# Attention and feed-forward on one core: scales from sums over partitions, and the last key tile's sigmoids as float16 parts lying over each other on partitions

## The chip, the cores and the metric

The kernel runs on one core of a Trainium2 chip. The metric is the device time of one execution, in microseconds, and lower is better. TensorE (PE in the profile) does the matmuls, VectorE (DVE) and ScalarE (ACT) the element-wise work, GpSimd (POOL) small scalings, and SyncE (SP) issues the DMAs.

## The reference, cut to what matters

```python
scores = (1 / sqrt(64)) * q @ k.transpose(0, 1, 3, 2) - log(448)      # q, k, v: (8, 12, 448, 64)
attn   = 1 / (1 + exp(-scores))                                       # a sigmoid, no softmax
x      = (attn @ v).transpose(0, 2, 1, 3).reshape(3584, 768)
h      = x @ w_in                                                     # 768 x 2048
g      = where(h > 0, h, exp(min(h, 0)) - 1)
out    = g @ w_out                                                    # 2048 x 768
```

All inputs and the output are float32.

## The kernel before, in words

A float32 matmul is replaced nearly everywhere by three float16 matmuls: each operand is scaled by a power of two and split into a high part (ScalarE, `nc.scalar.mul`) and a low part, the residual (VectorE, `scalar_tensor_tensor`), and high x high, low x high and high x low are accumulated. The helper `split` (L120) does both halves, so the profile shows them as L121 and L122 whatever the tile.

The work goes by batches (8) and within a batch by pairs of heads (6, `hp`). A pair's 448 keys are three tiles of 128 (`g` = 0 to 2) and a rest of 64 (`g` = NC = 3). For each tile there are `scores` (L384, into the PSUM tile `psc`), `soften` (the sigmoid L395 into `sg`, and for tiles 0 to 2 the split into `at`, L413 on ScalarE and L414 on VectorE) and `values` (L433: six float16 matmuls for a tile, each with 64 of the array's columns for one head, into `pav`). The rest tile has the 64 keys of both heads on one tile's 128 partitions: head 0 on 0 to 63, head 1 on 64 to 127. Its sigmoids stay float32, and one float32 matmul (L425) of 128x128 by 448 columns multiplies them with `vr`, in which the two heads' rest values stand as diagonal blocks, with zeros beside them; POOL makes `vr` (L360). The profile counts this matmul as two instructions. `finish` (L440, L441) splits `pav` into `xh` and takes its maximum.

`prepare` finds the powers of two for a later pair: absolute maxima along the rows of `rv`, the raw v, and of `raw`, which holds q and k (L300, L303; both show as L125), then the maximum over partitions in `magnitude`. That builds a diagonal matrix `dg` of the maxima, one for each of the three numbers (L105, VectorE), multiplies it with ones on TensorE (L110, 384 columns) so that each partition has all the maxima in a row, and reduces along the row (L112); L113 and L114 make a power of two of it. It returns in two further steps, `second` (the matmul and what follows) and `third` (the splits of q, k and v, and the DMA transpose).

Batch 0 (`EXACT` = 1) is done with float32 matmuls, while w_in is loaded and split beside it; w_out is loaded and split in batch 0's feed-forward and in the first pairs of batch 1. From batch 1 on the order on PE, ACT, DVE and SP is the order written (`manual_schedule`); before that a scheduler that simulates times orders the instructions. In the written order the pairs of batch b are mixed with the second feed-forward product of batch b - 1 (`moe2`, L529): `fill(n)` puts n steps of three matmuls between the parts of a pair. A batch has 96 such steps where b - 1 is even and 128 where it is odd, 16 or 21 for each pair. After the pairs comes the first product of batch b (`moe1`, L499), whose own scale goes through `magnitude` too (L457). One pair runs so:

```python
                for t in range(2):
                    p.scores(t)
                    p.soften(t)
                third()
...
                fill(gap)
                second = prepare_pair(n + 2)
                for t in range(2, NC + 1):
                    p.scores(t)
                    p.soften(t)
...
                fill(share - gap - tail)
                third = second()
                for t in range(NC + 1):
                    p.values(t)
                p.finish()
                fill(tail)
```

`gap` is 8 in a batch's first pair and 5 in the others, `tail` is 4 in its last pair and 0 in the others. In batch 1 the splitting of w_out (`step`) stands between the last `soften` and the second `fill` of the first three pairs. The output of a finished `moe2` tile leaves PSUM by L537.

Of the kernel before, what the change touches and what calls it, by code (L numbers as in the profile page):

```python
# [9 lines left out]
F16 = mybir.dt.float16  # L10
BF16 = mybir.dt.bfloat16
# [21 lines left out]
def attention_ffn(  # L33
# [64 lines left out]
    def magnitude(dst, mx, n):  # L98

        dg = sb.tile([P, n, P], BF16, tag="dg", name="dg", bufs=2)
        for i in range(n):
            nc.vector.tensor_scalar(dg[:, i], eye, mx[:, i : i + 1], None, op0=ALU.mult)  # L105

        def rest():
            pb = ps.tile([P, 512], F32, tag="pm", name="pb", bufs=3)
            row = pb[:, : n * P].rearrange("p (n x) -> p n x", x=P)
            nc.tensor.matmul(row, ones, dg, start=True, stop=True)  # L110
            al = sb.tile([P, n], F32, tag="al", name="al", bufs=2)
            nc.vector.tensor_reduce(al, row, axis=AX.X, op=ALU.max)  # L112
            nc.vector.tensor_scalar(al, al, TINY, None, op0=ALU.max)  # L113
            nc.vector.tensor_scalar(  # L114
                dst.bitcast(U32), al.bitcast(U32), 0x7F800000, None, op0=ALU.bitwise_and
            )
# [128 lines left out]
    def load_keys(dst, rest, src, b, h0):

        nc.sync.dma_start(
            dst.rearrange("p (h x) -> p h x", h=2),
            src[b, h0 : h0 + 2, :SM].rearrange("h (p c) d -> p h (c d)", c=NC),
        )  # L250
        for j in range(2):
            nc.sync.dma_start(rest[j], src[b, h0 + j, SM:])
# [17 lines left out]

    def load_v(b, hp):
        rv = rvs[(b * NP + hp) % len(rvs)]
        main = rv[:, : 2 * NC].rearrange("p t d -> p (t d)")
        load_keys(main, [rv[r, 2 * NC + j] for j, r in enumerate(rows)], v, b, 2 * hp)
        return rv

    def value_scale(b, hp, pv, c, xs):


        vm, vi = xs[:, 0], xs[:, 1]  # L280
        if hp:
            nc.vector.tensor_tensor(vm[:, hp : hp + 1], vm[:, hp - 1 : hp], pv, op=ALU.max)
        else:
            nc.gpsimd.tensor_copy(vm[:, 0:1], pv)
        nc.vector.reciprocal(vi[:, hp : hp + 1], vm[:, hp : hp + 1])
        if b < EXACT:
            nc.gpsimd.tensor_scalar(c, vi[:, hp : hp + 1], 2.0 ** (XTOP - 10), None, op0=ALU.mult)
        else:
            nc.gpsimd.tensor_scalar(
                c, vi[:, hp : hp + 1], pv, 2.0 ** (XTOP - 10 - TOP - ATOP),  # L290
                op0=ALU.mult, op1=ALU.mult,
            )

    def prepare(b, hp, raw, rv, xs):
# [1 line left out]

        u = f"{b}_{hp}"
        n = 1 if b < EXACT else 3
        mx = sb.tile([P, 3], F32, tag="mx", name=f"mx{u}", bufs=2)
        absmax(mx[:, 0:1], rv.rearrange("p t d -> p (t d)"))  # L300
        if n > 1:
            mt = sb.tile([P, 2, NC + 1], F32, tag="mt", name=f"mt{u}", bufs=2)
            absmax(  # L303
                mt.rearrange("p i t -> p (i t)")[:, : 2 * NC + 1],
                raw.rearrange("p t h d -> p t (h d)"),
            )
            nc.vector.tensor_reduce(mx[:, 1:3], mt[:, :, :NC], axis=AX.X, op=ALU.max)
            for i, r in enumerate(rows):
                m = mx[r, 1 + i : 2 + i]
                nc.vector.tensor_tensor(m, m, mt[r, 0, NC:], op=ALU.max)  # L310
# [20 lines left out]
        def transposed(sc):  # L331
            x_scale, s_rest, s_scale = (sc[:, n + i : n + i + 1] for i in range(3))
            if b < EXACT:
                pt = ps.tile([P, 2, 512], F32, tag="psc", name=f"pt{u}", bufs=2)
                pt = pt.rearrange("p a x -> p (a x)")
                for t in range(2 * NC + 1):
                    nc.tensor.transpose(
                        pt[:, t * P : (t + 1) * P], raw[:, t].rearrange("p h d -> p (h d)"), ident
                    )
                qk = early[:, hp % 2]  # L340
                nc.vector.tensor_copy(qk, pt[:, : 2 * S])
                return x_scale, 1 / math.sqrt(D), [qk], ([rv], rv[:, 2 * NC :])
# [12 lines left out]
            parts = [qk[:, i].rearrange("p t x -> p (t x)") for i in range(2)]  # L355

            vn = sb.tile([P, 2, 2 * NC, D], F16, tag="vn", name=f"vn{u}", bufs=2)
            split(vn[:, 0], vn[:, 1], rv[:, : 2 * NC], sc[:, 0:1])
            vr = sb.tile([P, 2, D], F32, tag="vr", name=f"vr{u}", bufs=2)
            nc.gpsimd.tensor_scalar(  # L360
                vr, rv[:, 2 * NC :], sc[:, 0:1], 2.0**ATOP, op0=ALU.mult, op1=ALU.mult
            )
            return x_scale, s_scale, parts, ([vn[:, 0], vn[:, 1]], vr)

        return scales

    class Pair:
# [23 lines left out]
        def soften(self, g):  # L391
# [6 lines left out]
            if b - 1 in last_exp:  # L398
# [8 lines left out]
            if b < EXACT or g == NC:  # L407
# [11 lines left out]
        def values(self, g):  # L419
            if g == 0:  # L420
                self.pav = ps.tile([P, 512], F32, tag="pav", name=f"pav{self.u}")
            pav, sg, (vv, vr) = self.pav, self.sg.pop(g), self.vs
            if g == NC:

                nc.tensor.matmul(  # L425
                    pav[:, :S], vr.rearrange("p t d -> p (t d)"), sg[0][:, 0],
                    start=False, stop=True,
                )
                return
            parts = [(0, 0), (1, 0), (0, 1)][: 2 * len(vv) - 1]  # L430
            for n, (i, k) in enumerate(parts):
                for j in range(2):
                    nc.tensor.matmul(  # L433
                        pav[rows[j], :S], vv[i][:, j * NC + g], sg[k][:, j],
                        start=(g == 0 and n == 0), stop=False,
                    )

        def finish(self):
# [4 lines left out]
    def rescale(b, xh, xs):  # L443


        vm, vi, xm = xs[:, 0], xs[:, 1], xs[:, 2]
        rr = sb.tile([P, NP + 3], F32, tag="rr", name=f"rr{b}", bufs=2)
        nc.vector.tensor_scalar(rr[:, :NP], vm, vi[:, NP - 1 :], None, op0=ALU.mult)
        for c in range(NP - 1):
            nc.vector.tensor_scalar(xh[:, c], xh[:, c], rr[:, c : c + 1], None, op0=ALU.mult)  # L450
        nc.vector.tensor_tensor(
            xm[:, : NP - 1], xm[:, : NP - 1], rr[:, : NP - 1], op=ALU.mult
        )
        yield
        mx, xp, xr = (rr[:, NP + i : NP + i + 1] for i in range(3))
        nc.vector.tensor_reduce(mx, xm, axis=AX.X, op=ALU.max)
        product = magnitude(xp, mx, 1)  # L457

        def rest():
            product()  # L460
            nc.vector.reciprocal(xr, xp)

        yield xp, xr, rest

    def moe_scales(m, xs, xr):

# [8 lines left out]
        nc.vector.tensor_scalar(m[:, 1], m[:, 1], xr, None, op0=ALU.mult)

# [69 lines left out]
    def out_scale(b, xs, xp, i=slice(0, NH)):  # L546
        if b % 2 == 0 and i.start == 0:
# [215 lines left out]
```

## Time and profile before

| what | value |
|---|---|
| median of 3 runs | 1271.27 us (1269.96 to 1274.96) |
| profiled execution, first to last instruction | 1269.1 us (no other time of this execution is given) |
| mean granted TensorE clock | 0.984 |
| TensorE, busy in matmuls | 1200.2 us, 95% |
| VectorE busy | 823.4 us, 65% |
| ScalarE busy | 671.8 us, 53% |
| POOL busy | 84.1 us, 7% |
| DMA, mean | 71 GB/s |

The span is the time between the first and the last instruction in the trace; the time of a run is measured around it. In a row of the order in time the first number is the start in us from the beginning of the span, the second the length of the row, which may gather several instructions (`x12`), then engine, line, operation and tiles; a bracket at the end gives idle time before the row and what ended it. PEld are the loads of the stationary operand, which can run beside matmuls. A matmul's shown length includes the time through the array, so the distance between two starts says what a matmul costs in a stream.

### The profile page before, as it was taken

How to read it: one execution, taken by the hardware profiler on the slowest of the kernel's cores; microseconds unless marked ns; L12 is line 12 of the kernel's file. 1: busy time of each engine (PE TensorE's matmuls, PEld its weight loads, DVE VectorE, ACT ScalarE, POOL GpSimd, SP SyncE). 2: the span in 40 equal slices, each digit the busy share in tenths (PEclk: the TensorE clock that was granted, in tenths of full speed). 3: DMA queues.
4: the chain of work that ended last, by engine and by line, in shares of the span. 5: the costliest groups of instructions: out<-in, count | busy, mean ns of one | idle time of the engine just before them, and what ended most of it. 6: DMA issues, size and time to landing. Idle time of an engine off the chain costs nothing.

```text
span 1269.1 us, 19337 instructions
## 1 busy us (share of the span) xinstructions
PE 1200.2 (95%) x7246; PEld 610.5 (48%) x7246; DVE 823.4 (65%) x1872; ACT 671.8 (53%) x1015; POOL 84.1 (7%) x319
## 2 busy tenths in 40 slices
PE   5979868999999999999999999999999999999998
PEld 2324334445555554545455554545455554455565
DVE  5898989765766557775666646885576656765500
ACT  5867777643655337744555436654565435663400
POOL 0011001100000000010000000010000100100000
PEclk9889979999999999999999999999999999999999
DMA  8937423420233103340144201440034401410000
GB/s 229 281 100 222 126 77 80 100 49 1 60 84 89 37 1 83 89 86 1 37 92 92 50 1 43 105 103 7 1 86 92 92 1 22 106 43 7 1 25 26
DMA packets 213407, 89.76 MB, mean 71 GB/s; under 512 B 177472, under 2 KB 209216, under 8 KB 213312
## 3 DMA queue, kind: packets, MB, share of 16 engines
q1 hardware_dynamic: 213312, 88.51, 28.7%
q8 instruction: 57, 0.93, 0.3%
q14 instruction: 38, 0.31, 0.1%
HBM read 58.20 MB, written 11.01 MB: 55 GB/s over the span
## 4 chain that ended last, share of the span: by engine, by line
PE 78%; ACT 8%; DVE 7%; DMA 3%; issue 2%; SPq 2%; DVEq 0%; POOL 0%; ACTq 0%; POOLq 0%
PE ph L499 31%; PE po L529 25%; PE psc L384 7%; PE pav L433 6%; PE po_r L529 5%; PE pav L425 3%; ACT sg L395 2%; DMA stage<-in_moe_w_in_dram 2%; ACT at L413 1%; SPq L262 1%; PE pb L110 1%; ACT L395 1%; ACT e L511 1%; DVE e L514 1%; DMA so<-in_moe_w_out_dram 1%
## 5 line engine op out<-in xcount | busy, mean ns | idle before, releaser
L499 PE MATMUL ph<-xh,wi 128*128 128x448 f16 x2304 | 442.0, 353 | 6.1 <-DVE xh L122 2.4
L529 PE MATMUL po<-wo,g 128*128 128x384 f16 x2304 | 392.9, 328 | 0.0
L529 PEld LDWEIGHTS <-g 128*128 128x128 f16 x2688 | 257.2, 98 | 198.4 <-issue 36.3
L499 PEld LDWEIGHTS <-wi 128*128 128x128 f16 x2304 | 225.3, 98 | 218.4 <-issue 7.6
L511 ACT ACTIVATE e<-ph,msc 128x448 f32<-128x448 f32 x128 | 80.8, 633 | 211.7 <-PE ph L499 211.6
L414 DVE SCALAR_TENSOR_TENSOR at<-sg,at 128x896 f16<-128x896 f32 x126 | 137.2, 1090 | 84.5 <-ACT at L413 84.5
L395 ACT ACTIVATE sg<-psc,bias,sc 128x896 f32<-128x896 f32 (+1 forms) x168 | 166.6, 992 | 1.7
L513 DVE TENSOR_SCALAR e<-e 128x448 f32<-128x448 f32 x128 | 50.3, 394 | 170.8 <-ACT e L511 170.7
L121 ACT ACTIVATE xh<-pav,sc 128x448 f16<-128x448 f32 x48 | 30.3, 632 | 216.7 <-PE pav L425 216.7
L384 PE MATMUL psc<-qk 64*128 64x448 f16 x1008 | 116.6, 355 | 11.4 <-ACT sg L395 11.4
L413 ACT ACTIVATE at<-sg 128x896 f16<-128x896 f32 x126 | 119.8, 951 | 4.1
L121 ACT ACTIVATE g<-e,msc 128x384 f16<-128x384 f32 (+1 forms) x192 | 96.0, 534 | 6.0 <-DVE e L514 4.3
L122 DVE SCALAR_TENSOR_TENSOR g<-e,msc,g 128x384 f16<-128x384 f32 (+1 forms) x192 | 94.6, 521 | 0.6
L514 DVE SCALAR_TENSOR_TENSOR e<-ph,msc,e 128x448 f32<-128x448 f32 x128 | 87.3, 683 | 4.0
L384 PEld LDWEIGHTS <-qk 64*128 64x128 f16 x1008 | 41.7, 97 | 89.7 <-issue 60.2
L433 PE MATMUL pav<-at,vn 128*64 128x448 f16 x756 | 80.2, 357 | 0.0
L324 POOL TENSOR_SCALAR sc<-pw 128x1 f32<-128x1 f32 x42 | 12.4, 295 | 843.5 <-DVE pw L114 790.9
L529 PE MATMUL po_r<-wo,g 128*128 128x384 f16 x384 | 64.7, 326 | 0.0
L122 DVE SCALAR_TENSOR_TENSOR xh<-pav,sc,xh 128x448 f16<-128x448 f32 x48 | 32.7, 680 | 48.7 <-ACT xh L121 48.7
L433 PEld LDWEIGHTS <-vn 128*64 128x64 f16 x756 | 39.4, 110 | 50.0 <-issue 27.8
L122 DVE SCALAR_TENSOR_TENSOR nat<-raw,sc,nat 128x384 f16<-128x384 f32 (+1 forms) x126 | 59.1, 524 | 0.0
L121 ACT ACTIVATE nat<-raw,sc 128x384 f16<-128x384 f32 (+1 forms) x126 | 58.8, 529 | 0.0
(103 smaller groups left out, 852.7 us busy)
## 6 DMA issues: line engine op xcount, KB each, us to landing
stage<-in_moe_w_in_dram SPq DMA_DIRECT2D x16, 768.0 KB, 6.6
raw<-in_q_dram SPq DMA_DIRECT2D x96, 96.0 KB, 3.1
raw<-in_k_dram SPq DMA_DIRECT2D x96, 96.0 KB, 2.6
rv<-in_v_dram SPq DMA_DIRECT2D x48, 192.0 KB, 2.7
out_dram<-o SPq DMA_DIRECT2D x48, 192.0 KB, 2.1
wo<-in_moe_w_out_dram SPq DMA_DIRECT2D x19, 384.0 KB, 4.1
so<-in_moe_w_out_dram SPq DMA_DIRECT2D x13, 384.0 KB, 4.3
raw<-in_q_dram SPq DMA_DIRECT2D x48, 32.0 KB, 2.4
```

The costliest lines, as they stand in the source:

```text
L121: nc.scalar.mul(hi, src, s)
L122: nc.vector.scalar_tensor_tensor(lo, src, s, hi, op0=ALU.mult, op1=ALU.subtract)
L384: nc.tensor.matmul(psc[:, j, :S] if g < NC else psc[rows[j], 0, :S], kk[rows[j], o], qq[rows[j], :S], start=(n == 0), stop=(n == len(parts ...
L395: a = nc.scalar.activation(sg[:, :nb], psc[:, :nb, :S], AF.Sigmoid, bias=bias, scale=self.s_scale)
L413: nc.scalar.mul(hi, sg, 2.0**ATOP)
L414: nc.vector.scalar_tensor_tensor(lo, sg, 2.0**ATOP, hi, op0=ALU.mult, op1=ALU.subtract)
L433: nc.tensor.matmul(pav[rows[j], :S], vv[i][:, j * NC + g], sg[k][:, j], start=(g == 0 and n == 0), stop=False,)
L499: nc.tensor.matmul(ph[:, :S], wi[:, wj, c, f * P : (f + 1) * P], xh[:, c, xj], start=(n == 0), stop=(n == 3 * NK - 1),)
L511: a = nc.scalar.activation(e, ph[:, :S], AF.Exp, scale=inv)
L513: nc.vector.tensor_scalar(e, e, 1.0, -1.0, op0=ALU.min, op1=ALU.add)
L514: nc.vector.scalar_tensor_tensor(e, ph[:, :S], inv, e, op0=ALU.mult, op1=ALU.max)
L529: nc.tensor.matmul(po[:, :HM], lh(gj, f), wo[:, i, f, wj], start=(n == 0), stop=(n == 3 * NF - 1),)
```

## The change

Four things are changed together.

- `magnitude` with its diagonals is replaced for the three numbers of `prepare` by `sums_of_rows`: the maxima (four columns for each number, bfloat16) are multiplied with ones directly, which gives their sums over the partitions, 12 columns in all (4 in batch 0), and the maximum is taken over the four. The q and k maxima are written straight into the columns of `mx`; the rest tile's maximum, which belongs to q on partitions 0 to 63 and to k on 64 to 127, is placed in two columns by one product with `half`, a matrix of two 0/1 columns. `moe1`'s scale keeps one diagonal (`greatest`), built from the float32 identity.
- The rest tile's sigmoids are split into float16 high and low parts in one tile `ar`: for head j the high part stands on the head's own 64 partitions, the low part on the other 64. The rest values of both heads are loaded twice, once to each half of the partitions, and split with the other values (8 blocks of 64 columns of `rv` in place of 6). A product over 128 partitions then sums high and low parts; the rest tile takes four float16 matmuls in place of the float32 one.
- In batch 0 the rest tile's one float32 matmul becomes two, each of 64 partitions by 64 columns of the array.
- A constant, 2^10 for the growth of x against its scale, becomes 2^3, because the sums are larger than the maxima.

```diff
+    half = const.tile([P, 2], BF16, name="half")
+    nc.vector.memset(half, 0.0)
+    nc.vector.memset(half[:R, 0:1], 1.0)
+    nc.vector.memset(half[R:, 1:2], 1.0)
...
-        nc.gpsimd.memset(rv[:, 2 * NC :], 0.0)
...
-        dg = sb.tile([P, n, P], BF16, tag="dg", name="dg", bufs=2)
-        for i in range(n):
-            nc.vector.tensor_scalar(dg[:, i], eye, mx[:, i : i + 1], None, op0=ALU.mult)
+    def sums_of_rows(dst, mx):
+        n = mx.shape[1]
         def rest():
-            pb = ps.tile([P, 512], F32, tag="pm", name="pb", bufs=3)
-            row = pb[:, : n * P].rearrange("p (n x) -> p n x", x=P)
-            nc.tensor.matmul(row, ones, dg, start=True, stop=True)
+            pb = ps.tile([P, 512], F32, tag="pm", name="pr", bufs=3)
+            sums = pb[:, : 4 * n].rearrange("p (n x) -> p n x", x=4)
+            nc.tensor.matmul(sums, ones, mx, start=True, stop=True)
             al = sb.tile([P, n], F32, tag="al", name="al", bufs=2)
-            nc.vector.tensor_reduce(al, row, axis=AX.X, op=ALU.max)
+            nc.vector.tensor_reduce(al, sums, axis=AX.X, op=ALU.max)
+            power_of_two(dst, al, TINY)
...
     def load_v(b, hp):
+        for r in rows:
+            nc.sync.dma_start(
+                rv[r, 2 * NC :], v[b, both, SM:].rearrange("h r d -> r h d")
+            )
...
     def prepare(b, hp, raw, rv, xs):
-        mx = sb.tile([P, 3], F32, tag="mx", name=f"mx{u}", bufs=2)
-        absmax(mx[:, 0:1], rv.rearrange("p t d -> p (t d)"))
+        mx = sb.tile([P, 15], BF16, tag="mx", name=f"mx{u}", bufs=2)
+        groups = mx.rearrange("p (n x) -> p n x", x=5)[:, :n, :4]
+        absmax(mx[:, 0:4], rv.rearrange("p (a t) d -> p a (t d)", a=4))
         if n > 1:
-            nc.vector.tensor_reduce(mx[:, 1:3], mt[:, :, :NC], axis=AX.X, op=ALU.max)
-            for i, r in enumerate(rows):
-                m = mx[r, 1 + i : 2 + i]
-                nc.vector.tensor_tensor(m, m, mt[r, 0, NC:], op=ALU.max)
+            absmax(mx[:, 6 : 2 * NC + 7], raw.rearrange("p t h d -> p t (h d)"))
+            nc.vector.tensor_tensor(
+                mx[:, 5:14:8], mx[:, 9:10].to_broadcast([P, 2]), half, op=ALU.mult
+            )
...
-            split(vn[:, 0], vn[:, 1], rv[:, : 2 * NC], sc[:, 0:1])
-            nc.gpsimd.tensor_scalar(
-                vr, rv[:, 2 * NC :], sc[:, 0:1], 2.0**ATOP, op0=ALU.mult, op1=ALU.mult
-            )
+            split(vn[:, 0], vn[:, 1], rv, sc[:, 0:1])
...
     def soften(self, g):
+            if g == NC:
+                ar = sb.tile([P, 2, S], F16, tag="ar", name=f"ar{self.u}")
+                for j, r in enumerate(rows):
+                    nc.scalar.mul(ar[r, j], sg[r, 0], 2.0**ATOP)
+                for j, r in enumerate(rows):
+                    nc.vector.scalar_tensor_tensor(
+                        ar[rows[1 - j], j], sg[r, 0], 2.0**ATOP, ar[r, j],
+                        op0=ALU.mult, op1=ALU.subtract,
+                    )
+                self.sg[g] = [ar]
+                return
...
     def values(self, g):
+            if g == NC and self.b < EXACT:
+                for j, r in enumerate(rows):
+                    nc.tensor.matmul(
+                        pav[r, :S], vv[0][r, 2 * NC + j], sg[0][r, 0], start=False, stop=True
+                    )
+                return
             if g == NC:
-                nc.tensor.matmul(
-                    pav[:, :S], vr.rearrange("p t d -> p (t d)"), sg[0][:, 0],
-                    start=False, stop=True,
-                )
-                return
+                parts = [(0, 0), (1, 0)]
...
                     nc.tensor.matmul(
-                        pav[rows[j], :S], vv[i][:, j * NC + g], sg[k][:, j],
-                        start=(g == 0 and n == 0), stop=False,
+                        pav[rows[j], :S],
+                        vv[i][:, 2 * NC + j if g == NC else j * NC + g], sg[k][:, j],
+                        start=(g == 0 and n == 0), stop=(g == NC and n == len(parts) - 1),
                     )
```

More of the change, by code (lines that the diff above doesn't have):

```diff
@@ L26 @@
 TINY = 2.0**-36
+XTINY = 2.0**-24
+XBITS = 3
 WTOP = 14
@@ L88, in attention_ffn @@
     nc.vector.memset(ones, 1.0)
-    eye = const.tile([P, P], BF16, name="eye")
-    nc.vector.tensor_copy(eye, ident)
+    half = const.tile([P, 2], BF16, name="half")
+    nc.vector.memset(half, 0.0)
+    nc.vector.memset(half[:R, 0:1], 1.0)
+    nc.vector.memset(half[R:, 1:2], 1.0)
     rvs = []
@@ L94, in attention_ffn, with power_of_two, greatest, rest @@
         rv = const.tile([P, 2 * NC + 2, D], F32, name=f"rv{i}")
-        nc.gpsimd.memset(rv[:, 2 * NC :], 0.0)
         rvs.append(rv)
-    def magnitude(dst, mx, n):
-        dg = sb.tile([P, n, P], BF16, tag="dg", name="dg", bufs=2)
-        for i in range(n):
-            nc.vector.tensor_scalar(dg[:, i], eye, mx[:, i : i + 1], None, op0=ALU.mult)
+    def power_of_two(dst, al, tiny):
+        nc.vector.tensor_scalar(al, al, tiny, None, op0=ALU.max)
+        nc.vector.tensor_scalar(
+            dst.bitcast(U32), al.bitcast(U32), 0x7F800000, None, op0=ALU.bitwise_and
+        )
+    def greatest(dst, mx):
+        dg = sb.tile([P, P], BF16, tag="dg", name="dg")
+        nc.vector.tensor_scalar(dg, ident, mx, None, op0=ALU.mult)
         def rest():
             pb = ps.tile([P, 512], F32, tag="pm", name="pb", bufs=3)
-            row = pb[:, : n * P].rearrange("p (n x) -> p n x", x=P)
-            nc.tensor.matmul(row, ones, dg, start=True, stop=True)
-            al = sb.tile([P, n], F32, tag="al", name="al", bufs=2)
[L112 to L115, printed above, removed]
-            )
+            nc.tensor.matmul(pb[:, :P], ones, dg, start=True, stop=True)
+            al = sb.tile([P, 1], F32, tag="al", name="al", bufs=2)
+            nc.vector.tensor_reduce(al, pb[:, :P], axis=AX.X, op=ALU.max)
+            power_of_two(dst, al, XTINY)
+        return rest
+    def sums_of_rows(dst, mx):
+        n = mx.shape[1]
+        def rest():
+            pb = ps.tile([P, 512], F32, tag="pm", name="pr", bufs=3)
+            sums = pb[:, : 4 * n].rearrange("p (n x) -> p n x", x=4)
+            nc.tensor.matmul(sums, ones, mx, start=True, stop=True)
+            al = sb.tile([P, n], F32, tag="al", name="al", bufs=2)
+            nc.vector.tensor_reduce(al, sums, axis=AX.X, op=ALU.max)
+            power_of_two(dst, al, TINY)
         return rest
@@ L243, in attention_ffn @@
     last_exp = {}
[L245 to L249, printed above, removed]
-        )
-        for j in range(2):
-            nc.sync.dma_start(rest[j], src[b, h0 + j, SM:])
     rows = [slice(0, R), slice(R, P)]
@@ L272, in load_v @@
         rv = rvs[(b * NP + hp) % len(rvs)]
-        main = rv[:, : 2 * NC].rearrange("p t d -> p (t d)")
-        load_keys(main, [rv[r, 2 * NC + j] for j, r in enumerate(rows)], v, b, 2 * hp)
+        both = slice(2 * hp, 2 * hp + 2)
+        nc.sync.dma_start(
+            rv[:, : 2 * NC].rearrange("p (h c) d -> p h (c d)", h=2),
+            v[b, both, :SM].rearrange("h (p c) d -> p h (c d)", c=NC),
+        )
+        for r in rows:
+            nc.sync.dma_start(
+                rv[r, 2 * NC :], v[b, both, SM:].rearrange("h r d -> r h d")
+            )
         return rv
@@ L298, in prepare @@
         n = 1 if b < EXACT else 3
-        mx = sb.tile([P, 3], F32, tag="mx", name=f"mx{u}", bufs=2)
-        absmax(mx[:, 0:1], rv.rearrange("p t d -> p (t d)"))
+        mx = sb.tile([P, 15], BF16, tag="mx", name=f"mx{u}", bufs=2)
+        groups = mx.rearrange("p (n x) -> p n x", x=5)[:, :n, :4]
+        absmax(mx[:, 0:4], rv.rearrange("p (a t) d -> p a (t d)", a=4))
         if n > 1:
[L302 to L305, printed above, removed]
-            )
-            nc.vector.tensor_reduce(mx[:, 1:3], mt[:, :, :NC], axis=AX.X, op=ALU.max)
-            for i, r in enumerate(rows):
-                m = mx[r, 1 + i : 2 + i]
-                nc.vector.tensor_tensor(m, m, mt[r, 0, NC:], op=ALU.max)
+            absmax(mx[:, 6 : 2 * NC + 7], raw.rearrange("p t h d -> p t (h d)"))
+            nc.vector.tensor_tensor(
+                mx[:, 5:14:8], mx[:, 9:10].to_broadcast([P, 2]), half, op=ALU.mult
+            )
         pw = sb.tile([P, n], F32, tag="pw", name=f"pw{u}", bufs=2)
-        product = magnitude(pw, mx[:, :n], n)
+        product = sums_of_rows(pw, groups)
         def scales():
@@ L355, in transposed @@
             parts = [qk[:, i].rearrange("p t x -> p (t x)") for i in range(2)]
[L357 to L363 removed]
+            vn = sb.tile([P, 2, 2 * NC + 2, D], F16, tag="vn", name=f"vn{u}", bufs=2)
+            split(vn[:, 0], vn[:, 1], rv, sc[:, 0:1])
+            return x_scale, s_scale, parts, [vn[:, 0], vn[:, 1]]
         return scales
@@ L421, in values @@
                 self.pav = ps.tile([P, 512], F32, tag="pav", name=f"pav{self.u}")
-            pav, sg, (vv, vr) = self.pav, self.sg.pop(g), self.vs
-            if g == NC:
-                nc.tensor.matmul(
-                    pav[:, :S], vr.rearrange("p t d -> p (t d)"), sg[0][:, 0],
-                    start=False, stop=True,
-                )
-                return
-            parts = [(0, 0), (1, 0), (0, 1)][: 2 * len(vv) - 1]
+            pav, sg, vv = self.pav, self.sg.pop(g), self.vs
+            if g == NC and self.b < EXACT:
+                for j, r in enumerate(rows):
+                    nc.tensor.matmul(
+                        pav[r, :S], vv[0][r, 2 * NC + j], sg[0][r, 0], start=False, stop=True
+                    )
+                return
+            if g == NC:
+                parts = [(0, 0), (1, 0)]
+            else:
+                parts = [(0, 0), (1, 0), (0, 1)][: 2 * len(vv) - 1]
             for n, (i, k) in enumerate(parts):
@@ L456, in rescale @@
         nc.vector.tensor_reduce(mx, xm, axis=AX.X, op=ALU.max)
-        product = magnitude(xp, mx, 1)
+        product = greatest(xp, mx)
         def rest():
```

14 lines of the change are left out of this document (7 added, 7 removed).

## The prediction

> **What bounds the kernel now.** I read the page's busy shares and its chain first, then the groups by shape, then the instructions in order of time around one attention pair, and last the waits. Columns of a group are count, busy us, mean ns of one, and idle before; of the order in time, start us, length us, engine.
>
> ```profile
> PE 1200.2 (95%) x7246; PEld 610.5 (48%) x7246; DVE 823.4 (65%) x1872; ACT 671.8 (53%) x1015; POOL 84.1 (7%) x319
> PE ph L499 31%; PE po L529 25%; PE psc L384 7%; PE pav L433 6%; PE po_r L529 5%; PE pav L425 3%; ACT sg L395 2%; DMA stage<-in_moe_w_in_dram 2%; ACT at L413 1%; SPq L262 1%; PE pb L110 1%; ACT L395 1%; ACT e L511 1%; DVE e L514 1%; DMA so<-in_moe_w_out_dram 1%
> L425 PE MATMUL pav<-sg,vr 128*128 128x448 f32 x84 | 43.6, 602 | 0.0
> ```
>
> TensorE sets the time: 95% busy, and nearly the whole chain is its lines. Two lines of the chain are rewritten, L425 (3%) and L110 (1%). The mean of a matmul has its pipeline in it, so I price by distances between starts. A pair of batch 3 (its fifth), which waits for nothing:
>
> ```profile
> 530.75 1.31 PE L384 MATMUL psc<-qk 64*128 64x448 f16 x12
> ...
> 530.86 0.64 ACT L121 ACTIVATE xh<-pav,sc 128x448 f16<-128x448 f32 x1 [4.54 <-PE pav L425]
> 531.21 1.14 SPq L252 DMA_DIRECT2D rv<-in_v_dram  x2
> ...
> 535.90 5.54 PE L529 MATMUL po<-wo,g 128*128 128x384 f16 x33
> ...
> 537.95 0.61 DVE L122 SCALAR_TENSOR_TENSOR vn<-rv,sc,vn 128x384 f16<-128x384 f32 x1
> 538.48 0.68 DVE L125 TENSOR_REDUCE mx<-rv 128x1 f32<-128x512 f32 x1
> 539.27 0.71 ACT L395 ACTIVATE sg<-psc,bias,sc 128x448 f32<-128x448 f32 x1
> 540.18 0.16 DVE L307 TENSOR_REDUCE mx<-mt 128x2 f32<-128x6 f32 x1
> 540.38 0.34 DVE L310 TENSOR_TENSOR mx<-mx,mt 64x1 f32<-64x1 f32 x2
> 540.75 0.58 DVE L105 TENSOR_SCALAR dg<-eye,mx 128x128 bf16<-128x128 bf16 x3
> 541.24 1.08 DVE L414 SCALAR_TENSOR_TENSOR at<-sg,at 128x896 f16<-128x896 f32 x1
> 541.38 0.32 PE L110 MATMUL pb<-dg,ones 128*128 128x384 bf16 x1
> 541.63 1.89 PE L433 MATMUL pav<-at,vn 128*64 128x448 f16 x18
> 542.25 0.61 DVE L537 TENSOR_SCALAR o<-po,osc 128x384 f32<-128x384 f32 x1
> 542.77 0.55 DVE L112 TENSOR_REDUCE al<-pb 128x3 f32<-128x384 f32 x1
> 543.46 1.02 PE L425 MATMUL pav<-sg,vr 128*128 128x448 f32 x2
> 543.54 0.62 SPq L266 DMA_DIRECT2D raw<-in_k_dram  x1
> 544.41 1.31 PE L384 MATMUL psc<-qk 64*128 64x448 f16 x12
> 544.51 0.63 ACT L121 ACTIVATE xh<-pav,sc 128x448 f16<-128x448 f32 x1 [4.54 <-PE pav L425]
> ```
>
> The period is 544.41 - 530.75 = 13.66 us, and TensorE fills it without a gap. ScalarE ends its work for the pair near 540 and waits 4.54 us for `pav`; VectorE is busy 10.39 us of it (length of the stretch; then busy us of PE, PEld, DVE, ACT, POOL; clock, DMA share, GB/s):
>
> ```profile
> 530.75:544.41 13.66, 13.66 (x94) 6.83 (x95) 10.39 (x22) 8.98 (x12) 1.51 (x8) 1.00 0.56 99
> ```
>
> **The change, part by part.**
>
> *The last value product (TensorE).* Now the float32 product runs from 543.46 to the next scores at 544.41, 0.95 us. The 18 float16 matmuls before it start at 541.63 and are through at 543.46: 1.83 us, so two matmuls (one on each half of the columns) go together, 0.203 us a couple, a change of tiling included. The new product is four of exactly this form, two couples: 0.41 us. Gain 0.95 - 0.41 = 0.54 us. The ends: nothing gained if the four ran one after the other (0.81 us plus a switch); 0.57 us if a couple costs its bare streaming time.
>
> The weight loads are the objection.
>
> ```profile
> L433 PEld LDWEIGHTS <-vn 128*64 128x64 f16 x756 | 39.4, 110 | 50.0 <-issue 27.8
> L529 PEld LDWEIGHTS <-g 128*128 128x128 f16 x2688 | 257.2, 98 | 198.4 <-issue 36.3
> ```
>
> A load of 64 columns takes 110 ns, one of 128 columns 98 ns; four exposed would cost 0.44 us. But 18 loads of 110 ns and 18 matmuls fit into 1.83 us together, so they lie beside the matmuls, and I keep 0.54. The Trainium skill, "TensorEngine Tiling (Array Packing)", Restrictions and Gotchas, says that column tiling excludes the fast weight load; the dearer load of half the width agrees with it, and where such loads were not hidden the sum would be rival C's. The same page, Key Properties, says that a change of tiling mode drains the engine; the change leaves out one such change in each pair, which lies in the 0.95 already.
>
> *The product for the scales (TensorE).* It has 384 columns now and gets 12 (4 in batch 0). No row has a matmul of 12 columns; the nearest is the one of 128 between matmuls of the same tiling:
>
> ```profile
> 563.33 0.22 PE L110 MATMUL pb<-dg,ones 128*128 128x128 bf16 x1
> 563.39 2.81 PE L499 MATMUL ph<-xh,wi 128*128 128x448 f16 x14
> ```
>
> It takes 0.06 us of the stream, and 384 columns take 0.166 (the 33 of L529 from 535.90 to 541.38), so of the 0.25 us from 541.38 to 541.63 about 0.09 is the switch. With 12 columns, 0 to 0.06 remains: gain 0.10 to 0.17, I take 0.13, near the row. By the Trainium skill (same page, Instruction Overhead: a matmul costs some 60 cycles however short) an estimate would be 25 ns, and the gain 0.135; no run here shows it.
>
> Together 0.67 us in a pair, if VectorE keeps up.
>
> *VectorE.* Away: L307 0.16, two L310 0.34, three L105 0.58, and most of L112. Added: one tiny product (0.16, as L307) and 128 more columns of `vn`, 0.12 (from 384 to 896 columns such an operation grows from 0.61 to 1.08, 0.92 ns a column). From L307 to L414 it is 541.24 - 540.18 = 1.06 us now and will be 0.16 + 0.03; with the 0.12, L414 of the third key tile starts 0.75 us earlier, at 540.49, and ends at 541.57. Behind it come the two new residuals of 64x448, which write the other half's partitions. The nearest rows:
>
> ```profile
> L122 DVE SCALAR_TENSOR_TENSOR g<-e,msc,g 128x448 f16<-128x448 f32 x64 | 43.2, 677 | 0.6
> L121 ACT ACTIVATE g<-e,msc 128x448 f16<-128x448 f32 x64 | 42.0, 660 | 3.6 <-DVE e L514 2.6 <-DVE msc L475 0.6
> L112 DVE TENSOR_REDUCE al<-pb 128x1 f32<-128x128 f32 x14 | 4.0, 288 | 16.8 <-PE pb L110 16.8
> ```
>
> Same types and columns, twice the partitions; L310 on 64 partitions is no cheaper than others of its size, so I take 0.68 each. The ends are 0.34 (time going with partitions) and 1.08 (the row of twice the columns). The second ends at 541.57 + 1.36 = 542.93. TensorE gets to the product that needs it at 541.38 + 0.12 + 1.70 = 543.2: hidden, with 0.27 us to spare. Queued behind are L537 and L112; L112 over 12 columns is about 0.17 us (0.55 for 384 and 0.288 for 128 make 1.03 ns a column). They end near 544.4, when ScalarE's `xh` (543.8 + 0.63) releases the next VectorE work. VectorE's sum is +1.36 + 0.16 + 0.12 - 0.16 - 0.34 - 0.58 - 0.38 = +0.2 us in 13.0.
>
> *ScalarE.* Two multiplications of 0.66 after the sigmoid that ends at 539.98, and 0.1 for the longer `vn`: done near 541.4, ahead of VectorE's turn and of `xh`. Hidden by the 4.54 us of waiting; without that cover 1.4 us a pair.
>
> *POOL, SP, DMA.* `vr` on POOL goes; nothing waited on it. The two rest loads of `v` (1.14 us of SP for two) take the shape of L266's, 0.62 each: +0.1 us in SP's queue, in front of the next pair's loads only, which are issued a whole pair before they are used. 32 KB more per pair; no wait of the quoted pair is for `rv`.
>
> *Six pairs where TensorE waits for the diagonals.*
>
> ```profile
> PE pb L110 <- DVE dg L105: 11.6, 6, 2.0
> 549.55 3.59 PE L529 MATMUL po<-wo,g 128*128 128x384 f16 x21
> ...
> 554.91 1.09 DVE L414 SCALAR_TENSOR_TENSOR at<-sg,at 128x896 f16<-128x896 f32 x1
> 555.05 0.32 PE L110 MATMUL pb<-dg,ones 128*128 128x384 bf16 x1 [1.91 <-DVE dg L105]
> ...
> 557.98 2.11 PE L529 MATMUL po<-wo,g 128*128 128x384 f16 x12
> ```
>
> Here VectorE sets the time. The diagonals go, but what is late next is the second residual: L414 ends at 556.00 - 0.75 = 555.25, the residuals at 556.61, then a matmul, another couple and the switch, 0.1 + 0.2 + 0.2: 557.15 in place of 557.98. Gain 0.83.
>
> *First pair of batch 1.* The splitting of w_out comes behind, on ScalarE and VectorE, and TensorE ends up waiting for it:
>
> ```profile
> 187.90 1.14 DVE L122 SCALAR_TENSOR_TENSOR wo<-wo,swo 128x384 f16<-128x384 f32 x2
> 196.46 0.74 PE L384 MATMUL psc<-qk 64*128 64x448 f16 x6 [2.51 <-ACT sg L395]
> ```
>
> That work begins -0.75 + 1.36 = 0.6 us later, and the wait passes it on: +0.6 there.
>
> *Batch 0 and the weights (0 to 187 us).* Not TensorE's time but loads, ScalarE and VectorE in turn. The float32 product of the last tile becomes two on opposite quarters of the array; four instructions of that form take what two of the full form take:
>
> ```profile
> 35.89 0.97 PE L384 MATMUL psc<-early 64*64 64x448 f32 x4
> 39.26 0.96 PE L425 MATMUL pav<-sg,rv 128*128 128x448 f32 x2
> ```
>
> So nothing (ends: 0 and +0.75 a pair, beside other work). VectorE loses a diagonal (0.25) and about 0.12 of L112 in each pair, and 1.3 in each of the two pairs prepared there for batch 1: 5 us less where it is often the bound, against more bytes in a stretch with the DMA engines full. The order there is planned anew, so -5 to +8; I take -1.
>
> *The sum.* Of 42 pairs, 33 are regular: 33 x 0.67 = 22.1. Two (the last of batch 7) prepare nothing: 2 x 0.54 = 1.1. Six at 0.83: 5.0. One at -0.6. Before them 1.0. Together 28.6 us: the profiled span of 1269.1 becomes 1240.5. The median of the runs (1271.27) lies 2.2 us above that span; so 1242.7, say 1243 us.
>
> **The rivals.**
>
> A, the forecast: 1243, on its own 1237 to 1249.
>
> B, VectorE becomes the bound. The spare time is only 0.27 us. For it: each regular pair of the odd batches has this tight fit; against it: no row of that shape above 0.68. At 1.08 each, the second residual ends at 543.73, the next scores start at 544.2 instead of 543.74, and 0.2 of the gain stays in 15 regular pairs; the 18 of the even batches have 21 steps of filling in place of 16 (15 matmuls more, 2.5 us) and keep 0.67; the six gain nothing. 3 + 12 + 1 - 1.4 + 1 = 16: about 1255.
>
> C, exposed weight loads: 0.67 - 0.44 = 0.23 a regular pair: 7.6 + 0.2 + 2.3 - 0.6 + 1 = 10.5, about 1261.
>
> D, the first 187 us replanned to the worse by some 8 us, or to the better by 5: 1252, or 1239.
>
> E, slower: writing to the other half's partitions costs VectorE much more. With the 0.48 us that the last couple, its matmul and the switch take, it decides from 541.57 + 2t + 0.48 = 544.41 on, t = 1.18 us. At t = 1.7 the 15 tight pairs lose 1.04 each, the six about 1.2, the first pair 2.6, while the even batches keep 12: 15.6 + 7.2 + 2.6 - 12 - 1 = +12, 1283. No row is near that.
>
> F, the change does not do what it says (TensorE's gain returns as another wait in each pair): 1271. The 0.27 us speak for some of it, the free ScalarE and the filling against all of it.
>
> **How the numbers follow.** A 0.68, D 0.12 (worse 0.08, better 0.04), B 0.09, C 0.05, E 0.03, F 0.03. The range 1234 to 1256 holds A, B and D; C, E and F are left out. Within 0.5% (6.4 us, about what a measurement tells here) is F and a weak C: 0.04. Slower is E: 0.03. Faster: 0.93.
>
> **What would show it.** In the same kind of pair of the profile after: a period near 13.0 us; 22 matmuls of `pav` without the float32 pair, about 2.24 us to the next scores; the matmul for the scales about 0.12 us ahead of them; two residuals of about 0.68 us ending before the last four matmuls begin; no wait on diagonals except once a batch; 1.4 us more of ScalarE. It would be wrong if `pav` waited for the residuals in ordinary pairs, if a couple took much over 0.2 us, or if the stretch up to 187 us changed by more than 5.

## The result and the profile after

The changed kernel takes 1236.68 us (median of 4 runs, 1235.33 to 1238.24), the kernel before 1273.05 us on the same occasion; the ratio is 0.9722, 95% interval 0.9702 to 0.9741. Run again beside four of the experiments it took 1237.17 us against 1273.06 us, 0.9715 (0.9699 to 0.9732). So the change is worth about 36 us where 28 were forecast; the time lies inside the range of 1234 to 1256 and 0.3 us below the own range of the likeliest case (1237 to 1249). The profiled execution has a span of 1236.5 us, 32.6 us less than that of before.

From the page of the changed kernel: busy shares, and the lines of the chain that ended last.

```profile
PE 1170.5 (95%) x7342; PEld 605.9 (49%) x7342; DVE 828.8 (67%) x1742; ACT 725.2 (59%) x1099; POOL 71.8 (6%) x275
PE ph L520 32%; PE po L550 26%; PE psc L390 8%; PE pav L453 7%; PE po_r L550 5%; ACT sg L401 2%; DMA stage<-in_moe_w_in_dram 2%; ACT at L430 1%; DVE mx L140 1%; DMA wo<-in_moe_w_out_dram 1%; ACT L401 1%; DVE at L431 1%; DVE nat L137 1%; DVE ar L422 1%; DVE e L535 1%
```

TensorE is still 95% busy: it has 29.7 us less to do, and the span is shorter by as much and a little more. The float32 product of the rest tile and the matmul for the scales are gone from the chain. VectorE has 5 us more work, ScalarE 53 us more. L520, L550, L390, L453 and L401 are the lines L499, L529, L384, L433 and L395 of before.

The same pair as in the prediction (the fifth of batch 3), in order of time:

```profile
519.88 1.31 PE L390 MATMUL psc<-qk 64*128 64x448 f16 x12
...
525.02 5.54 PE L550 MATMUL po<-wo,g 128*128 128x384 f16 x33
...
527.07 0.75 DVE L137 SCALAR_TENSOR_TENSOR vn<-rv,sc,vn 128x512 f16<-128x512 f32 x1
...
529.24 1.17 ACT L420 ACTIVATE ar<-sg 64x448 f16<-64x448 f32 x2
529.45 0.17 DVE L318 TENSOR_TENSOR mx<-mx,half 128x2 bf16<-128x2 bf16 x1
529.52 1.08 DVE L431 SCALAR_TENSOR_TENSOR at<-sg,at 128x896 f16<-128x896 f32 x1
...
530.39 0.17 PE L128 MATMUL pr<-mx,ones 128*128 128x12 bf16 x1
530.50 1.89 PE L453 MATMUL pav<-at,vn 128*64 128x448 f16 x18
530.64 1.27 DVE L422 SCALAR_TENSOR_TENSOR ar<-sg,ar 64x448 f16<-64x448 f32 x2
531.94 0.62 DVE L558 TENSOR_SCALAR o<-po,osc 128x384 f32<-128x384 f32 x1
532.22 0.55 PE L453 MATMUL pav<-ar,vn 128*64 128x448 f16 x4
532.48 0.16 DVE L130 TENSOR_REDUCE al<-pr 128x3 f32<-128x12 f32 x1
...
532.70 1.31 PE L390 MATMUL psc<-qk 64*128 64x448 f16 x12
532.81 0.64 ACT L136 ACTIVATE xh<-pav,sc 128x448 f16<-128x448 f32 x1 [2.40 <-PE pav L453]
```

The period is 532.70 - 519.88 = 12.82 us instead of 13.66. The matmul for the scales costs 0.11 us of the stream (530.39 to 530.50) instead of 0.25, the whole of `pav` 2.20 us (530.50 to 532.70) instead of 2.78. The second residual ends at 531.91, 0.31 us before the four matmuls on `ar` begin. ScalarE's wait for `pav` has shrunk from 4.54 to 2.40 us and still covers the two multiplications.

The costs of the new operations, from the groups by shape:

```profile
L422 DVE SCALAR_TENSOR_TENSOR ar<-sg,ar 64x448 f16<-64x448 f32 x84 | 52.1, 620 | 2.8
L420 ACT ACTIVATE ar<-sg 64x448 f16<-64x448 f32 x84 | 48.3, 575 | 2.4
L130 DVE TENSOR_REDUCE al<-pr 128x3 f32<-128x12 f32 x42 | 6.9, 163 | 6.0 <-PE pr L128 6.0
L128 PE MATMUL pr<-mx,ones 128*128 128x12 bf16 x42 | 7.2, 171 | 6.6 <-DVE mx L318 6.6
```

To compare kernels I take from each trace the distance between the first `pav` matmuls of successive pairs (or from the first `ph` matmul of the feed-forward). From batch 2 on, the distance at one place of the order repeats from batch to batch to 0.01 us, wherever TensorE's clock is full:

| distance, us | before | after | e1 | e2 | e3 | e4 | e6 |
|---|---|---|---|---|---|---|---|
| pair to pair, 16 steps of filling | 13.66 | 12.82 | 13.39 | 13.53 | 13.89 | 13.20 | 13.00 |
| pair to pair, 21 steps | 15.98 | 15.26 | 15.83 | 15.41 | 15.26 | 15.64 | 15.44 |
| fifth to last pair, batches 1, 3, 5 | 13.66 | 12.09 | 12.53 | 13.53 | 13.16 | 12.47 | 12.27 |
| last pair to `ph`, batches 3, 5 | 4.63 | 4.63 | 4.63 | 4.47 | 5.96 | 5.01 | 4.45 |
| `ph` to first pair, batches 3, 5, 7 | 68.64 | 67.64 | 67.50 | 68.76 | 67.64 | 67.63 | 67.82 |
| first to second pair, batch 3 | 13.66 | 13.29 | 13.39 | 13.53 | 14.62 | 13.67 | 13.29 |
| first to second pair, batch 1 | 19.06 | 21.18 | 19.09 | 21.60 | 19.44 | 19.50 | 19.49 |
| first `pav` of batch 1, at | 187.32 | 186.26 | 185.15 | 190.54 | 186.46 | 185.69 | 185.41 |

### The profile page after: what moved, and what is told of

It reads as the page before. It is cut to its first block, busy times and chain, and to the rows that moved or that the text cites. A ratio compares the mean times of both kernels' runs of the same rounds, so it can differ in the third digit from the quotient of the medians.

```text
span 1236.5 us, 19394 instructions
## 1 busy us (share of the span) xinstructions
PE 1170.5 (95%) x7342; PEld 605.9 (49%) x7342; DVE 828.8 (67%) x1742; ACT 725.2 (59%) x1099; POOL 71.8 (6%) x275
## 4 chain that ended last, share of the span: by engine, by line
PE 78%; DVE 8%; ACT 7%; DMA 3%; issue 2%; SPq 1%; POOL 0%; DVEq 0%; ACTq 0%
PE ph L520 32%; PE po L550 26%; PE psc L390 8%; PE pav L453 7%; PE po_r L550 5%; ACT sg L401 2%; DMA stage<-in_moe_w_in_dram 2%; ACT at L430 1%; DVE mx L140 1%; DMA wo<-in_moe_w_out_dram 1%; ACT L401 1%; DVE at L431 1%; DVE nat L137 1%; DVE ar L422 1%; DVE e L535 1%
## 5 line engine op out<-in xcount | busy, mean ns | idle before, releaser
L520 PE MATMUL ph<-xh,wi 128*128 128x448 f16 x2304 | 443.5, 354 | 7.1 <-DVE xh L471 4.2
L550 PE MATMUL po<-wo,g 128*128 128x384 f16 x2304 | 392.7, 328 | 0.0
L550 PEld LDWEIGHTS <-g 128*128 128x128 f16 x2688 | 256.5, 98 | 197.5 <-issue 35.2
L520 PEld LDWEIGHTS <-wi 128*128 128x128 f16 x2304 | 225.7, 98 | 221.2 <-issue 11.1
L401 ACT ACTIVATE sg<-psc,bias,sc 128x896 f32<-128x896 f32 (+1 forms) x168 | 166.6, 992 | 1.5
L390 PE MATMUL psc<-qk 64*128 64x448 f16 x1008 | 117.8, 356 | 12.5 <-ACT sg L401 12.5
L390 PEld LDWEIGHTS <-qk 64*128 64x128 f16 x1008 | 41.9, 97 | 81.3 <-issue 58.9
L453 PE MATMUL pav<-at,vn 128*64 128x448 f16 x756 | 79.5, 355 | 0.0
L453 PEld LDWEIGHTS <-vn 128*64 128x64 f16 x924 | 48.8, 109 | 46.6 <-issue 18.5
L550 PE MATMUL po_r<-wo,g 128*128 128x384 f16 x384 | 64.8, 326 | 0.0
L558 DVE TENSOR_SCALAR o<-po,osc 128x384 f32<-128x384 f32 x48 | 29.6, 617 | 41.5 <-PE po L550 35.8
```

The source lines that it names most:

```text
L390: nc.tensor.matmul(psc[:, j, :S] if g < NC else psc[rows[j], 0, :S], kk[rows[j], o], qq[rows[j], :S], start=(n == 0), stop=(n == len(parts ...
L401: a = nc.scalar.activation(sg[:, :nb], psc[:, :nb, :S], AF.Sigmoid, bias=bias, scale=self.s_scale)
L453: nc.tensor.matmul(pav[rows[j], :S], vv[i][:, 2 * NC + j if g == NC else j * NC + g], sg[k][:, j], start=(g == 0 and n == 0), stop=(g == N ...
L520: nc.tensor.matmul(ph[:, :S], wi[:, wj, c, f * P : (f + 1) * P], xh[:, c, xj], start=(n == 0), stop=(n == 3 * NK - 1),)
L550: nc.tensor.matmul(po[:, :HM], lh(gj, f), wo[:, i, f, wj], start=(n == 0), stop=(n == 3 * NF - 1),)
```

## The experiments

Medians and ratios of each kernel to the kernel before, run beside it:

| run | median, us | before, us | ratio, 95% interval |
|---|---|---|---|
| e1_sums_only | 1254.75 | 1274.28 | 0.9845 (0.9825 to 0.9865) |
| e2_parts_only | 1261.79 | 1274.28 | 0.9900 (0.9882 to 0.9919) |
| e3_residuals_twice | 1264.71 | 1274.28 | 0.9925 (0.9910 to 0.9940) |
| e4_couples_twice | 1252.47 | 1274.28 | 0.9841 (0.9816 to 0.9865) |
| after_again | 1237.17 | 1273.06 | 0.9715 (0.9699 to 0.9732) |
| e6_wide_sums | 1241.82 | 1273.06 | 0.9760 (0.9745 to 0.9775) |
| e7_before_no_idle | 1270.32 | 1273.06 | 0.9983 (0.9970 to 0.9996) |
| e8_steps_later | 1234.34 | 1273.06 | 0.9699 (0.9684 to 0.9713) |
| e9_tail | 1231.71 | 1273.84 | 0.9676 (0.9657 to 0.9694) |

The theory (T): TensorE's stream sets the period, VectorE has a few tenths of a microsecond to spare in a pair with 16 steps, and the two parts of the change need each other. The rival: TensorE's savings are independent, and VectorE's work is hidden.

### One part alone

e1 keeps the scales by sums and puts the rest tile back:

```diff
-                ar = sb.tile([P, 2, S], F16, tag="ar", name=f"ar{self.u}")
-                ... (multiplications, residuals, four float16 matmuls)
+                self.sg[g] = [sg]     # and one float32 matmul with vr, as before
```

> The change's scales from sums over partitions, with the rest tile, its float32 product and vr as before the change. Theory T (TensorE pays by stream distance; the short product saves 0.15 us in 40 pairs, the diagonals' 0.11 us of hidden wait in 15 pairs, and about 1 us in each of the six pairs that wait for the diagonals): 6 + 1.7 + 6, and about 1 before batch 1: 14 to 15 us faster than before, about 1258. Rival (the sums save their columns only): 6 us, about 1267.

It is 19.5 us faster than before, more than either said. The sums save 0.15 us in a pair with 21 steps, which is the short matmul, but 0.27 us with 16: there the diagonals had delayed TensorE by 0.12 us without any idle time in the trace. The pairs that waited gain more: 1.13 us from the fifth to the last pair and 1.14 us ahead of the first. With the 2.2 us up to the first pair of batch 1, and the clock lost in the profiled execution of before (below), these make up the 17 us between the profiled spans.

e2 keeps the parts and puts the diagonals back:

```diff
-        product = sums_of_rows(pw, groups)
+        product = magnitude(pw, mx[:, :n], n)
...
-                ar = sb.tile([P, 2, S], F16, tag="ar", name=f"ar{self.u}")
+                ar = sg[:, 1].bitcast(F16).rearrange("p (j s) -> p j s", j=2)
```

> The change's float16 parts of the rest tile, with the scales by diagonals as before the change; ar lies in the unused half of the tile sg. Theory T (VectorE has only about 0.3 us to spare in a pair with 16 steps of filling, and that only since the diagonals are gone): the second residual ends about 0.45 us too late in 15 pairs, the six waiting pairs gain nothing, so 42 x 0.57 - 15 x 0.5 - 6 x 0.57 - 1 = 12 us faster than before, about 1261; this and e1 add up to less than the whole change by some 9 us. Rival (the parts are independent): the whole change less e1, 21 to 22 us faster, about 1251.

12.5 us faster, as T had it. In the pairs with 21 steps the parts are worth 0.57 us, with 16 only 0.13, and ahead of the first pair, where TensorE waits for the diagonals, nothing (68.76 instead of 68.64). The trace shows why, around one `pav` of a pair with 16 steps (here `ar` has the name of `sg`):

```profile
543.29 0.58 DVE L106 TENSOR_SCALAR dg<-eye,mx 128x128 bf16<-128x128 bf16 x3
543.79 1.08 DVE L420 SCALAR_TENSOR_TENSOR at<-sg,at 128x896 f16<-128x896 f32 x1
543.92 0.32 PE L111 MATMUL pb<-dg,ones 128*128 128x384 bf16 x1
...
544.90 1.27 DVE L411 SCALAR_TENSOR_TENSOR sg<-sg 64x448 f16<-64x448 f32 x2
545.90 0.35 PE L442 MATMUL pav<-sg,vn 128*64 128x448 f16 x1
```

The diagonals push the residuals back to 544.90; they end at 546.17, when TensorE has done one of the four matmuls and stands. In the pairs with 16 steps the parts alone are worth 0.13 and the sums alone 0.27 us, together 0.84; with 21 steps they simply add up (0.57 + 0.15 = 0.72). That is the interaction: by removing VectorE's diagonals the sums pay for the residuals. Over the whole kernel it is smaller than T had it: the medians of e1 and e2 gain 19.5 + 12.5 = 32.0 us, some 4 less than the change's 36, where T had 9; the profiled executions gain 17.1 + 7.9 = 25.0 of 32.6, as that of e2 lost 5.8 us up to and in the first pair of batch 1.

### The residuals on VectorE

```diff
+                    for _ in range(2):
                         nc.vector.scalar_tensor_tensor(
                             ar[rows[1 - j], j], sg[r, 0], 2.0**ATOP, ar[r, j],
```

> The changed kernel, with each of the two residuals of the rest tile computed twice on VectorE (1.27 us more in each of 42 pairs). Theory T: 15 pairs with 16 steps lose 1.27 - 0.3, six waiting ones and the first of batch 1 lose 1.27, the pairs with 21 steps nothing: 14.5 + 9 = 23 us slower than the changed kernel, about 1260. Rival (the residuals lie wholly beside TensorE's work): no change, about 1237.

28 us slower than the changed kernel's 1236.7 to 1237.2, which were taken on other occasions; between the profiled executions it is 26.9. The four residuals take 2.58 us in the trace where two took 1.27. These 1.31 us more on VectorE cost 1.07 us in a pair with 16 steps, so 0.24 us was to spare (0.27 in the prediction); with 21 steps they cost nothing, 15.26 as in the changed kernel. The wait stands in the trace:

```profile
541.10 1.89 PE L454 MATMUL pav<-at,vn 128*64 128x448 f16 x18
541.24 2.58 DVE L423 SCALAR_TENSOR_TENSOR ar<-sg,ar 64x448 f16<-64x448 f32 x4
542.83 0.35 PE L454 MATMUL pav<-ar,vn 128*64 128x448 f16 x1
543.87 0.57 PE L454 MATMUL pav<-ar,vn 128*64 128x448 f16 x3 [0.69 <-DVE ar L423]
```

What goes beyond T's 23 us is mostly in the batches with 21 steps, where T had no cost: from their first to their second pair it is 0.65 us longer (15.91), and from the last pair to `ph` 0.44 us (4.60).

### The matmuls of the rest tile

```diff
-                parts = [(0, 0), (1, 0)]
+                parts = [(0, 0), (1, 0), (0, 0), (1, 0)]
```

> The changed kernel, with the four float16 matmuls of the rest tile done twice (the output counts the rest keys twice). Theory T (two matmuls on the two halves of the columns go together, a couple costs 0.19 to 0.20 us, the loads lie beside): 42 x 0.39 = 16 us slower than the changed kernel, about 1253. Rival (the matmuls go one after the other, or their loads show): 0.8 us a pair, 34 us slower, about 1271.

0.38 us in the regular pairs of both kinds, 0.19 a couple. In all it is 15 to 16 us by medians of different occasions, and 13.2 between the profiled executions, in which the first pair of batch 1 was 1.7 us shorter. So two matmuls on the two halves of the columns do go together, and their loads are hidden: four of them, 110 ns each, would alone be 0.44 us. Rival C is out.

### The width of the matmul for the scales

```diff
-            nc.tensor.matmul(sums, ones, mx, start=True, stop=True)
+            nc.tensor.matmul(wide, ones, mx.unsqueeze(1).to_broadcast([P, 32, n, 4]), start=True, stop=True)
```

> The changed kernel, with the matmul for the scales over 384 columns again (the 12 columns read 32 times), and no diagonals. Theory T (each column of it is paid on TensorE): 0.15 us in each of 40 pairs, 6 us slower than the changed kernel. Rival (only the diagonals mattered, the columns lie in the switch of tiling): no change.

0.18 us in a regular pair of either kind, 0.48 ns a column. So the columns are paid, and not the diagonals alone. The whole kernel loses 4.7 us rather than the 6 of T: the first pair of batch 1 was 1.7 us shorter in this execution, and from the first to the second pair of batches 3, 5 and 7 nothing changed, since there TensorE waits for the residuals on VectorE. The matmul and the values behind it:

```profile
530.00 0.35 PE L130 MATMUL pr<-mx,ones 128*128 128x384 bf16 x1
530.29 1.89 PE L459 MATMUL pav<-at,vn 128*64 128x448 f16 x18
```

### The clock in the kernel before

In the profiled execution of before, one of the six waits for the diagonals (1.97 us, in batch 5) is followed by 3.4 us at half the granted clock, which is the column before the last two; the number behind the comma is TensorE's busy time in the window:

```profile
778.86:782.27 3.41, 1.44 (x15) 0.62 (x14) 3.28 (x9) 0.76 (x2) 0.00 (x0) 1.00 0.86 171
782.27:785.69 3.42, 3.42 (x14) 1.04 (x12) 1.41 (x7) 0.00 (x0) 1.12 (x5) 0.51 0.58 128
785.69:789.10 3.41, 3.41 (x26) 1.81 (x27) 1.77 (x3) 3.27 (x4) 0.38 (x1) 1.00 0.29 95
```

Over the 8 us from 780 to 788 the mean is the 0.79 of the expectation below. In batch 5 the step from first to second pair was 15.26 us instead of 13.66. In the changed kernel no window between 208 us and the last 2 us is below full clock. e7 fills the waits of before with matmuls whose result is overwritten:

```diff
             pb = ps.tile([P, 512], F32, tag="pm", name="pb", bufs=3)
+            for k in range(busy):     # 10 in the six pairs, 0 elsewhere
+                nc.tensor.matmul(pb[:, :HM], ones, wi[:, 0, 0, :HM].bitcast(BF16), start=True, stop=True)
```

> The kernel before, with ten idle matmuls of 384 columns (1.6 us, their result is overwritten) put into the six waits of 1.9 us for the diagonals, so that TensorE is not idle there. Theory T (some of these waits let the granted clock fall to about 0.79 for 8 us, 1.6 us lost each time, in a number that differs from run to run): no low clock after 210 us in the trace, the median 2 to 4 us below that of the kernel before. Rival (the spread of the kernel before has another source): the same median as the kernel before.

From batch 2 on the distances between pairs are those of before, but no window after 208 us is below full clock in the profiled execution, and the median is 2.7 us lower, an interval that just excludes no change (0.9970 to 0.9996). One of the filled waits:

```profile
485.17 1.79 PE L110 MATMUL pb<-wi,ones 128*128 128x384 bf16 x10
487.30 0.32 PE L114 MATMUL pb<-dg,ones 128*128 128x384 bf16 x1 [0.34 <-DVE dg L105]
```

So a wait of TensorE can cost twice here: once as a wait, and now and then again as clock. It happened once more after a wait of this length, in e2, where the clock was 0.50 from 266.99 to 270.40. Ahead of that fall TensorE was busy for 1.38 of 3.41 us; around an equally long wait in batch 3 of before, after which the clock stayed at 1.00, it was 1.96 of 3.40:

```profile
263.58:266.99 3.41, 1.38 (x14) 0.65 (x14) 3.24 (x9) 1.84 (x4) 0.00 (x0) 1.00 0.90 179
485.30:488.70 3.40, 1.96 (x19) 0.93 (x18) 3.25 (x10) 0.04 (x1) 0.00 (x0) 1.00 0.81 163
```

The runs of e7 still spread over 5 us, so this is not the only source of spread.

### Two mends that the traces pointed to

In the first pair of batch 1 TensorE waited 4.22 us for a sigmoid that stands on ScalarE behind splits of w_out, and ran at half clock for 6.8 us from the end of it (changed kernel; the second and third rows are windows of 4 us, clock in the column before the last two):

```profile
197.02 1.30 PE L390 MATMUL psc<-qk 64*128 64x448 f16 x6 [4.22 <-ACT sg L401]
196.00:200.00 4.00, 2.31 (x12) 0.82 (x11) 3.60 (x12) 3.94 (x5) 1.17 (x5) 0.62 0.13 49
200.00:204.00 4.00, 4.00 (x15) 1.84 (x14) 4.00 (x7) 3.97 (x7) 0.00 (x0) 0.53 0.09 18
```

```diff
-                    step(3 if hp < NC - 1 else NF)
+                    step((0, 3, NF)[hp])
```

> The changed kernel, with three splits of w_out moved from the first pair of batch 1 to the third (0, 3 and the rest in place of 3, 3 and the rest). Theory T (there the splits stand before ScalarE's next xh, and TensorE waits 4.2 us for the sigmoid behind it and then runs at half clock): the wait falls by some 2 us, with the clock 2 to 4 us faster than the changed kernel. Rival (the wait is passed on to the third pair): no change.

1234.34 us, 2.8 us below the changed kernel beside it. The first step of batch 1 is 16.37 us instead of 21.21, with no low clock behind it, but the three after it are 13.28, 13.35 and 13.10 instead of 12.82: about 1.3 us is passed on, the rest is kept. e9 adds a shorter tail:

```diff
-                tail = 4 if hp == NP - 1 else 0
+                tail = (2 if b % 2 and b < B - 1 else 4) if hp == NP - 1 else 0
```

> The changed kernel with the later splits of w_out (0, 3 and the rest) and, in the last pair of batches 1, 3 and 5, two steps of filling after the values in place of four, so two more before. Theory T (in these pairs TensorE waits 1.06 us for the maxima and some 0.4 us for the residuals; 0.98 us of work moved ahead of them fills that): 0.7 to 1 us in each of three batches, 2 to 3 us faster than with the later splits alone, 1231 to 1233. Rival (the scaling of xh on VectorE ends as late as before, and the first feed-forward product then waits for it): no change, 1234 to 1235.

1231.71 us, 2.6 us below e8 (run on another occasion), ratio to before 0.9676. In the last pairs it is less than the 0.7 to 1 us of T. From the last pair to `ph` it is 3.65 us instead of 4.63, and from `ph` to the next pair 69.36 instead of 68.97: 0.6 us a batch is kept, since the feed-forward's own scale now makes TensorE wait a little:

```profile
544.25 0.22 PE L114 MATMUL pb<-dg,ones 128*128 128x128 bf16 x1 [0.21 <-DVE dg L110]
```

That makes 1.8 us in three batches. The rest of the 2.6 us is not the tail's: two medians of the kernel before, on these two occasions, differ by 0.8 us too (1273.06 and 1273.84). e9 is faster than both the kernel before and the changed one.

## Why the prediction came out as it did

By its own sum, against the profiled executions (28.6 us forecast, 32.6 measured):

- **The last value product**, 0.54 forecast. e2 and e4 give 0.57 and 0.19 a couple: right, at its upper end, which was the bare streaming time.
- **The matmul for the scales**, 0.13 forecast, 0.15 measured (e1, pairs with 21 steps). The gap to the values is 0.11 us with 12 columns. The 60 cycles that the Trainium skill's "TensorEngine Tiling (Array Packing)" gives for a short matmul (Instruction Overhead), 25 ns, with the 0.09 us of the switch make an estimate of 0.115, and this trace agrees. It does not decide it: 12 columns at the 0.48 ns of e6 would make 0.10.
- **Regular pairs with 16 steps**, 0.67 forecast, 0.84 measured: the largest error, 15 pairs, 2.6 us. The step that failed is "waits for nothing" and "TensorE fills it without a gap". In the trace of before the diagonals end at 540.75 + 0.58 = 541.33 and the matmul that reads them starts at 541.38; e1 shows that 0.12 us of that pair was a wait, and e6, which has the 384 columns without the diagonals, agrees (33 matmuls in 5.37 us). It could not be seen as idle time, because the shown length of the last `po` matmul covers it. It could have been seen in the steps: 33 matmuls in 5.48 us before, 5.37 us after. The remaining 0.05 us are the value product at its upper end and the short matmul. The 18 pairs with 21 steps, which had no such wait, measured 0.72 for the same 0.67, 0.9 us in all.
- **The six waiting pairs**, 0.83 forecast, about 1.05 measured (the batches 3 and 5 gain 5.43 us without the clock, of which four pairs are 3.36). The mechanism was right: the wait for the maxima fell from 1.9 to 1.06 us in a batch's last pair (1.97 to 1.13 in its first), and the residuals are late next. A residual takes 0.62 us instead of 0.68, and 1.27 us for two.

```profile
542.49 0.17 PE L128 MATMUL pr<-mx,ones 128*128 128x12 bf16 x1 [1.06 <-DVE mx L318]
...
543.46 1.27 DVE L422 SCALAR_TENSOR_TENSOR ar<-sg,ar 64x448 f16<-64x448 f32 x2
544.32 1.01 PE L453 MATMUL pav<-ar,vn 128*64 128x448 f16 x4
```

The last row's four matmuls, 0.55 us in other pairs, spread over 1.01 us: they wait for the second residual.

- **The first pair of batch 1**, 0.6 lost by forecast, 2.1 in this execution. The later start of the splits was as forecast (188.46 instead of 187.90 on VectorE), and the sigmoid that TensorE waits for came 0.56 us later (197.02 instead of 196.46). But TensorE had begun the pair 1.06 us earlier and only waited longer, 4.22 instead of 2.51 us, and the stretch behind the wait took 0.5 us more, with half clock for 6.8 us instead of 3.4. It is not a fixed price: the same distance was 19.1 to 21.6 us in the kernels of the table.
- **Up to the first pair of batch 1**, 1.0 gained by forecast, 1.1 measured; the kernels of the table lie within 5.4 us of each other there, so this agreement is luck. And the gain did not reach the end: it went into the wait just named. The two terms, added up as a gain of 0.4 us, came to a loss of 1.1.
- **The clock** was no term at all. The lost 1.6 us in batch 5 of before came back. The rest between the 32.6 us of the two profiled executions and the 36.4 us of the medians is their place among the runs: the profiled execution of before was shorter than the median of its kernel, that of after longer (1238.24 us).

So the time fell inside the stated range, but below A's own: the hidden wait and the clock were not in its sum, the six pairs were put too low, and the first pair of batch 1 took some of it back. VectorE's slack, on which rival B rested, was 0.24 us where 0.27 was forecast: e3 shows that B was near, and e2 that without the sums it would have come true.

## What to carry to other kernels

When two edits meet on a second engine, price them together: here one edit's VectorE time was paid for with what the other freed, and each alone was worth 0.13 and 0.27 us in a pair instead of 0.84. Where an instruction starts right at the end of what it reads (0.05 us behind it here), suspect a wait even if the profile shows no idle time, and check the stream's rate just ahead of it. A wait of two microseconds on TensorE can be worth removing for its clock too.

## What the hardware showed that was not expected

- A wait of 2 us can halve TensorE's granted clock for 3.4 us, and what seems to count is how much of it falls into one stretch of 3.41 us. After 208 us the profiled executions show two such falls, in before and in e2. If time is cut into stretches of 3.41 us counted from the falls, the ones just ahead of them are the two in which TensorE was busy least, 42% and 40%; no other from there on, the last few microseconds aside, was under 50%. Where the limit lies is not shown: before 208 us, stretches of 42 to 53% were followed by half clock in some cases and by full clock in others. The Trainium skill, "TensorE: Matmul & The Clock Gate", Part 1, puts the fall to half clock after at least one idle window of about 3.4 us, free-running. The length agrees with these traces, but here TensorE was not idle for the whole of it.
- Writing a residual to the other half's partitions took 620 ns for 64x448, less than the 677 ns of the 128x448 row that it was priced by. No run has the same operation on its own half, so what the move itself costs is not shown; it is not much.
